# A recurrent attention with a max-out feed-forward on one core: the planner that orders the instructions gets other transfer rules and other due times

## The chip, the cores and the metric

One core of a Trainium2 chip. The metric is the device time of one launch in microseconds, median of several runs. Times that come from a view of the profile belong to one profiled execution.

## What is computed

The reference, cut to what matters. B, H, S, D are 4, 8, 768, 48:

```python
for t in range(S):
    cur = einsum('bhd,bhe->bhde', u * k[t], v[t])
    y[t] = einsum('bhd,bhde->bhe', r[t], state + cur)
    state = w * state + einsum('bhd,bhe->bhde', k[t], v[t])
x = y as (3072 tokens) x 384
h = max(x @ w1, x @ w2, x @ w3)          # 384 -> 768
out = h @ w_out                          # 768 -> 384
```

All inputs are float32. The kernel carries most products as pairs of 16-bit numbers, a high part and a low part.

## The kernel before

**Tiling.** The sequence is cut into 12 chunks of 64 positions. A chunk has two halves q of four heads each, so attention has 24 half-steps. A half-step loads `feat` (k and r, turned so that features lie on partitions; 512 KB) and `tok` (k, r and v by token; 576 KB), scales k and r by powers of the decay, and makes three groups of small matmuls on TensorE (line 438): *scores* (24 matmuls), *keys* (24, they update the state) and *values* (48, they give the chunk's x). The feed-forward (FFN) of a chunk follows: 162 matmuls *up* and 54 *down* (line 516), on 256 tokens, with ACT taking the first of three products, DVE the maximum with the other two (line 531), ACT the high part of h (line 534) and POOL or DVE its low part (line 540).

**Spread copies.** TensorE takes the 16-bit weights of attention as block-diagonal tiles. ACT writes the high part and DVE the low part into a dense tile (`kd`, `ktd`, `vd`, `sd`, lines 357, 362 and 364), and two DMAs on SP's queue (lines 344 and 345) copy its upper and lower partitions to the spread tile (`kb`, `ktb`, `vb`, `sb`). `kb` and `ktb`, and their dense tiles, exist once and serve both halves; `vb` and `sb` once for each half. `feat` has 2 buffers, `tok` 4. The scaled k lies in feat's own buffer, so `high` (line 357) and `low` (line 362) of k read that buffer.

**What sets the order.** Nothing is ordered by a scheduler at build time: every piece of work is given to `Plan.do` with an engine, a cost, what it reads and writes and a due time, and `Plan.order` runs a small model of the engines and of the DMA pipe. At each step it takes, of the pieces that could start soonest, the one with the least due time. The result is the order in which the instructions are issued, engine by engine; each engine works through its own list in that order, and SP through its DMAs. Two tables move due times: `SHIFT` by kind of work and by stage of the program (start, chunks up to 4, the rest), `ONCE` for single pieces. The model frees a buffer when the last piece that names it among what it reads, writes or takes is done.

In the model of before, a DMA of size bytes goes through one pipe of 275 GB/s, with 1.5 us before and 0.9 us behind; a pair of spread copies counts as one transfer. The pieces `kdh` and `kdl` (high and low of k) name the scaled k but not feat's buffer, so the model may free that buffer ahead of them. The program itself always waits for them: the next load into that buffer is held back until line 362 has read it.

**The rest.** At the start the eight weight tiles are loaded in sixteen halves and cut into high and low parts on ACT and DVE; near the end the sixteen halves are read again and vetted (lines 288 and 292), and all vets and sums of squares end in a flag that decides whether a slow general path runs.

Of the kernel before, what the change touches and what calls it, by code (L numbers as in the profile page):

```python
# [19 lines left out]
C = 64  # L20
# [5 lines left out]
U = 8  # L26
# [16 lines left out]
class Plan:  # L43
# [4 lines left out]
    ISSUE = {"sp": 0.45, "act": 0.45, "pool": 1.0}  # L48
    RATE, BEFORE, BEHIND = 275e3, 1.5, 0.9
    STAGES = (1.6, 4)  # L50
    SHIFT = {
        "act ah": (-52.95, 14.65, 8.9), "act am": (7.15, -25.65, 17.2), "act hh": (-9.55, -32.05, -3.85),
        "act his": (13, 6.75, -11.8), "act io": (-16.6, -18, 1.9), "act kb": (-22.35, -8.1, 1.25),
        "act kdh": (-90.3, 16.35, 22), "act ktb": (-2.95, -2, 18.3), "act ktdh": (17.9, 2.35, 12.8),
        "act m": (-43.35, -37.2, -5), "act odd": (-37.5, -41.9, 2.15), "act rh": (4.2, 20.15, -18.95),
        "act sdh": (-69.4, 17.1, -6.65), "act sq": (9.1, 22.1, -1.4), "act sqw": (52.2, 1.25, 16.95),
        "act sqx": (1.2, -35.65, -16.7), "act state": (-11.95, -53.65, -0.65), "act tkt": (-25.15, -0.3, 3.45),
        "act vb": (-38.6, 6.95, 36.75), "act vdh": (-6.55, 4.75, 38.8), "act xh": (-48.5, 27.05, 13.05),
        "act ztop": (-87.85, -53.05, -29.95), "dve a": (-2.75, 32.75, 52), "dve al": (25.3, -21.5, -38.65),
        "dve am": (-41.8, 17.75, -13.55), "dve ends": (5.75, 45, -4.95), "dve flag": (47.55, 0.5, -27.95),  # L60
        "dve good": (9.65, -41.8, 12.85), "dve hl": (13.7, -19.15, -51.75), "dve kT": (-41.9, 48, -0.3),
        "dve kdec": (17.3, 22.7, 20.85), "dve kdl": (-77.2, 31.3, -20.35), "dve ktdl": (-24.55, -30, -24.95),
        "dve lo": (-26.5, -32.1, 20.85), "dve m": (-48.25, -37.75, 4.15), "dve rT": (46.55, 22.2, 29.7),
        "dve rl": (-4.2, -8.6, 21.2), "dve sdl": (-11.9, 2.05, 25.1), "dve state": (-5.65, 12.5, 19.6),
        "dve vdl": (-13.05, 11.4, 22.45), "dve vet": (18.2, -10.95, 35.4), "dve word": (-32.05, 8.5, 49.3),
# [3 lines left out]
        "pool hl": (23.4, -2.9, -15.95), "pool kT": (6.85, -26.05, 38.8), "pool kdec": (2, -20.25, 12.7),  # L69
# [3 lines left out]
    }  # L73
    ONCE = {
        "act am": {3: -5.5}, "act his": {2: -61.15}, "act ktb": {1: -45.5}, "act ktdh": {3: -20.5},
        "act rh": {5: -30.5, 7: 29}, "act sdh": {3: 70}, "act sq": {3: -57, 5: -57, 6: -57.75, 39: -15}, "act xh": {0: 56.5},
        "act ztop": {3: 41.5}, "dve a": {2: -66.3}, "dve al": {4: -17}, "dve am": {5: -28.5, 6: -29.5, 8: -27.5},
        "dve hl": {2: -6}, "dve kT": {2: -29.5, 3: -27.5}, "dve kdec": {2: -86}, "dve ktdl": {8: 86.5},
        "dve lo": {3: -45, 4: -45, 5: -44.5, 6: 32.5}, "dve m": {13: 39.5}, "dve rT": {2: -117.5, 3: -116},
        "dve rl": {0: -65, 1: -63}, "dve sdl": {1: -57.5}, "dve state": {4: -25.5},  # L80
        "dve vdl": {0: -56, 2: 15, 5: -54.5, 6: -38.5}, "dve word": {4: -39.5, 5: -39.5, 6: -37}, "dve xl": {12: -39},
# [9 lines left out]
    def do(self, due, eng, cost, fn, reads=(), writes=(), takes=(), size=0, near=0):  # L91


        n = len(self.todo)
# [15 lines left out]
        self.todo.append(dict(n=n, due=due, eng=eng, cost=cost, fn=fn, need=need, takes=takes, size=size, near=near, kind=kind, touch={*reads, *writes, *new}))  # L110

    def order(self, free):

        free, pipe = dict(free), 0.0
# [14 lines left out]
        def earliest(p):  # L129
            t = free[p["eng"]]  # L130
            for m in p["need"]:
                q = self.todo[m]
                t = max(t, end[m] if q["eng"] != p["eng"] or q["size"] and not p["size"] else start[m] + busy[m] + (0 if p["size"] else 0.06))
            for pool, _ in p["takes"]:
                old = taken[pool]
                if len(old) >= self.bufs[pool]:
                    k = old[len(old) - self.bufs[pool]]
                    if left[k]:
                        return None
                    t = max(t, gone[k])  # L140
            return t

        while ready:
# [12 lines left out]
            start[n], free[e] = t, t + cost  # L156
            busy[n] = cost
            if p["size"]:
                pipe = max(pipe, t + p["cost"] + self.BEFORE) + p["size"] / self.RATE
                end[n] = pipe + self.BEHIND  # L160
            else:
                end[n] = t + cost + self.LAG[e]
# [16 lines left out]
def kernel(ctx, tc, feat, tok, wu, ut, ws, wo, cst, out):  # L179
# [514 lines left out]
    def dma(due, fn, size, reads=(), writes=(), takes=(), eng="sp", n=1):  # L694
        do(due, eng, n * Plan.ISSUE[eng], fn, reads, writes, takes, size)

# [40 lines left out]
    def before_scores(c, q, due):  # L737
# [5 lines left out]
        do(due - 0.26, "act", act(U * C), lambda: high(kd, u(raws[c, q]["kT"]), C), reads=[("kT", c, q)], writes=["kdh"])  # L743
        do(due - 0.24, "dve", dve(U * C), lambda: low(kd, u(raws[c, q]["kT"]), C), reads=[("kT", c, q), "kdh"], writes=["kdl"], near=1.2)
# [255 lines left out]
```

## Time and profile before

| what | value |
|---|---|
| median of 3 runs | 426.75 us (426.45 to 429.45) |
| the profiled execution | 427.69 us |
| its span, first to last instruction | 425.9 us |
| mean granted TensorE clock | 0.976 |
| instructions | 12008 |
| moved by DMA | 90.08 MB, mean 211 GB/s |

How to read the views: *idle* is the time of an engine ahead of an instruction, put down to what released it last. `PE` is matmul, `PEld` weight load, `SPq` the queue of DMAs that SP issues, `L438` a line of the kernel. `PE psa` is attention's work on TensorE, `PE psm` that of the FFN. In the groups of DMA issues the last number is the median time from the issue to the landing.

### The profile page before, as it was taken

The page shows a single profiled execution, that of the slowest core. Times are in us where ns is not written, and L with a number is a line of the kernel's source. Part 1 is how long each engine was busy: PE and PEld are TensorE (multiplying, and loading weights), DVE is VectorE, ACT ScalarE, POOL GpSimd, SP SyncE. Part 2 cuts the span into 40 slices and gives each one's busy share as a digit, 9 for nine tenths or more (in the row PEclk, how much of TensorE's full clock was granted, in tenths as well). Part 3 has the DMA queues.
Part 4 walks back from the last instruction along what each step waited for, and adds up shares of the span by engine and source line. Part 5 has one row for each costly group of instructions (what it writes and reads, how often), then busy time and mean ns, then how long its engine had stood idle before and what let it go on. Part 6 is the DMA issues. An engine that isn't in the chain of part 4 may idle for free.

```text
span 425.9 us, 12008 instructions
## 1 busy us (share of the span) xinstructions
PE 377.8 (89%) x4758; PEld 335.8 (79%) x4758; DVE 284.7 (67%) x550; ACT 274.9 (65%) x714; POOL 178.2 (42%) x180
## 2 busy tenths in 40 slices
PE   2969899989499999799898986986998999999995
PEld 2967679978389899788787875875887899888884
DVE  5889999896369678998683584574497643434340
ACT  5999988967266776685683574474476444689621
POOL 9000001495355288588467348526455501111020
PEclk9999999999979999999999898899999999999999
DMA  8956999976888996799879759649786793518101
GB/s 288 415 175 201 270 311 272 282 214 190 201 198 237 265 299 158 195 278 255 250 204 239 244 135 278 180 139 254 200 245 174 193 343 111 171 45 240 68 2 41
DMA packets 30954, 90.08 MB, mean 211 GB/s; under 512 B 4784, under 2 KB 9648, under 8 KB 30896
## 3 DMA queue, kind: packets, MB, share of 16 engines
q1 hardware_dynamic: 25568, 84.47, 68.9%
q10 hardware_dynamic: 5328, 4.82, 3.5%
q8 instruction: 38, 0.62, 0.6%
q14 instruction: 20, 0.16, 0.1%
HBM read 45.85 MB, written 4.72 MB: 119 GB/s over the span
## 4 chain that ended last, share of the span: by engine, by line
PE 35%; DMA 27%; DVE 16%; ACT 10%; issue 6%; POOL 2%; SPq 2%; ACTq 1%; DVEq 0%; POOLq 0%
PE psm L516 29%; DMA ktb<-ktd 10%; DMA kb<-kd 8%; PE psa L438 5%; DMA tok<-in_tok_dram 4%; ACT junk L378 3%; DVE m L531 2%; DMA out_dram<-io 2%; DVE w L276 2%; DMA feat<-in_feat_dram 2%; DVE raw L269 1%; DVE kd L362 1%; DVE al L458 1%; ACT ztop L265 1%; DVE feat L395 1%
## 5 line engine op out<-in xcount | busy, mean ns | idle before, releaser
L516 PEld LDWEIGHTS <-w 128*128 128x128 f16 x2592 | 253.7, 99 | 44.4 <-issue 10.0
L516 PE MATMUL psm<-xh,w 128*128 128x256 f16 x1296 | 228.6, 277 | 3.9 <-ACT xh L494 1.7
L516 PE MATMUL psm<-xl,w 128*128 128x256 f16 x648 | 157.6, 278 | 2.3 <-DVE xl L499 2.2
L540 POOL TENSOR_TENSOR hl<-m,hh 128x256 f16<-128x256 f32 x55 | 41.0, 748 | 164.0 <-ACT hh L534 162.7
L531 DVE SCALAR_TENSOR_TENSOR m<-psm,m 128x256 f32<-128x256 f32 x144 | 60.3, 420 | 52.2 <-PE psm L516 38.3
L395 POOL TENSOR_TENSOR feat<-feat,wrt 128x512 f32<-128x512 f32 x36 | 50.5, 1413 | 35.7 <-DMA feat<-in_feat_dram 35.7
L516 PE MATMUL psm<-hh,w 128*128 128x256 f16 x432 | 56.7, 275 | 2.3 <-ACT hh L534 2.3
L378 ACT ACTIVATE junk<-tok 128x384 bf16<-128x384 f32 x72 | 37.4, 520 | 26.4 <-DMA tok<-in_tok_dram 25.5
L534 ACT CAST hh<-m 128x256 f16<-128x256 f32 x72 | 28.5, 399 | 27.7 <-DVE m L531 27.0
L438 PE MATMUL psa<-al,vb 128*128 128x64 f16 x176 | 31.2, 193 | 3.8 <-DVE al L458 3.8
L516 PE MATMUL psm<-hl,w 128*128 128x256 f16 x216 | 34.0, 277 | 0.2
L438 PE MATMUL psa<-ah,vb 128*128 128x64 f16 x352 | 33.3, 193 | 0.3 <-ACT ah L453 0.3
L438 PEld LDWEIGHTS <-vb 128*128 128x128 f16 x528 | 29.2, 98 | 5.2 <-issue 4.7
L438 PE MATMUL psa<-rh,sb 128*128 128x64 f16 x352 | 32.5, 193 | 0.0
L438 PE MATMUL psa<-vd,ktb 128*128 128x48 f16 x480 | 16.2, 187 | 18.0 <-DMA ktb<-ktd 17.9
L527 ACT ACTIVATE m<-psm 128x256 f32<-128x256 f32 x72 | 26.9, 376 | 7.6 <-PE psm L516 7.3
L499 DVE SCALAR_TENSOR_TENSOR xl<-psa,xh 32x256 f16<-32x256 f32 (+2 forms) x60 | 28.3, 471 | 5.2 <-ACT xh L494 4.4
L494 ACT ACTIVATE xh<-psa 32x256 f16<-32x256 f32 (+2 forms) x60 | 24.9, 415 | 9.9 <-PE psa L438 4.4
L438 PE MATMUL psa<-rl,sb 128*128 128x64 f16 x176 | 31.2, 193 | 0.0
L405 DVE TENSOR_TENSOR rl<-feat,rh 128x512 f16<-128x512 f32 x22 | 21.8, 990 | 13.9 <-ACT rh L400 13.9
L438 PEld LDWEIGHTS <-ktb 128*128 128x128 f16 x480 | 15.0, 98 | 20.4 <-issue 12.0
L414 POOL TENSOR_TENSOR am<-tok,u_sb 128x384 f32<-128x384 f32 x18 | 20.0, 1109 | 24.0 <-DVE al L458 23.3
(93 smaller groups left out, 591.4 us busy)
## 6 DMA issues: line engine op xcount, KB each, us to landing
tok<-in_tok_dram SPq DMA_DIRECT2D x24, 576.0 KB, 7.2
raw<-in_ws_dram SPq DMA_DIRECT2D x24, 576.0 KB, 7.4
feat<-in_feat_dram SPq DMA_DIRECT2D x24, 512.0 KB, 4.5
kb<-kd SPq DMA_DIRECT2D x22, 256.0 KB, 6.9
kb<-kd SPq DMA_DIRECT2D x22, 248.0 KB, 6.8
ktb<-ktd SPq DMA_DIRECT2D x20, 256.0 KB, 6.7
ktb<-ktd SPq DMA_DIRECT2D x20, 248.0 KB, 7.1
raw<-in_wo_dram SPq DMA_DIRECT2D x8, 576.0 KB, 7.1
```

What stands on the lines that cost most here:

```text
L378: nc.scalar.activation(out=dst, in_=src, func=AF.Square, scale=scale, accum_out=stat[:, at:at + 1])
L395: helper(c).tensor_tensor(out=t[n], in0=t[n], in1=tb, op=ALU.mult)
L405: nc.vector.tensor_tensor(out=t["rl"], in0=units(t["rT"]), in1=t["rh"], op=ALU.subtract)
L414: helper(c).tensor_tensor(out=w.rearrange("p (g b) d -> p g b d", g=2), in0=t["r"], in1=by_token(u_sb, q), op=ALU.mult)
L438: nc.tensor.matmul(out=ps, lhsT=l[i], rhs=rr[j], start=first and n == 0, stop=last and n == 2)
L494: nc.scalar.mul(out=hi, in_=src, mul=SC_X)
L499: nc.vector.scalar_tensor_tensor(out=lo, in0=src, scalar=SC_X, in1=hi, op0=ALU.mult, op1=ALU.subtract)
L516: nc.tensor.matmul(out=ps, lhsT=a, rhs=b, start=first and n == 0, stop=last and n == len(prods) - 1)
L527: nc.scalar.mul(out=m, in_=ps, mul=SC_M)
L531: nc.vector.scalar_tensor_tensor(out=m, in0=ps, scalar=SC_M, in1=m, op0=ALU.mult, op1=ALU.max)
L534: nc.scalar.copy(out=h[0][:, f, :], in_=m)
L540: lows_by(c, f).tensor_tensor(out=h[1][:, f, :], in0=m, in1=h[0][:, f, :], op=ALU.subtract)
```

## The change

The change is in the planner and in what three pieces declare; no instruction is added or taken away. (1) `high` and `low` of k now name feat's buffer among what they read. (2) At most eight transfers are under way in the model: a DMA starts no sooner than the eighth before it has ended, and the two copies of a spread are modelled one by one. (3) The rates differ by kind: 300 GB/s for loads, 220 for spreads, 500 for stores; issue costs and the times before and behind are a little smaller. (4) Both tables of due times are new, and due times are rounded to whole steps of 0.0001 before they are compared. The diff, with one row of each table:

```diff
-    ISSUE = {"sp": 0.45, "act": 0.45, "pool": 1.0}
-    RATE, BEFORE, BEHIND = 275e3, 1.5, 0.9
+    ISSUE = {1: 0.4, 2: 1.1}
+    LOAD, SPREAD, STORE = 300e3, 220e3, 500e3
+    BEFORE, BEHIND, LANES = 1.3, 0.8, 8
...
-        "act ah": (-52.95, 14.65, 8.9), "act am": (7.15, -25.65, 17.2), "act hh": (-9.55, -32.05, -3.85),
+        "act ah": (-9.7, -6.55, -15.55), "act am": (-7.65, -25.3, 6.4), "act hh": (-8.7, -29.65, -23.6),
...
-        "sp word": {1: 0.05, 8: -0.1},
+        "pe va": {4: -10, 10: -1.5, 16: -0.3}, "sp word": {9: -0.2, 10: 0.1, 14: -0.12},
...
-    def do(self, due, eng, cost, fn, reads=(), writes=(), takes=(), size=0, near=0):
+    def do(self, due, eng, cost, fn, reads=(), writes=(), takes=(), size=0, near=0, parts=1):
...
-        self.todo.append(dict(n=n, due=due, eng=eng, ...
+        self.todo.append(dict(n=n, due=math.floor(due * 1e4 + 0.5), eng=eng, ...
...
-        free, pipe = dict(free), 0.0
+        free, pipe, lanes = dict(free), 0.0, [0.0] * self.LANES
...
+            if p["size"]:
+                t = max(t, lanes[-self.LANES])
...
-            start[n], free[e] = t, t + cost
-            busy[n] = cost
-            if p["size"]:
-                pipe = max(pipe, t + p["cost"] + self.BEFORE) + p["size"] / self.RATE
-                end[n] = pipe + self.BEHIND
-            else:
-                end[n] = t + cost + self.LAG[e]
+            start[n], now = t, t
+            for _ in range(p["parts"] if p["size"] else 0):
+                now = max(now, lanes[-self.LANES]) + cost / p["parts"]
+                pipe = max(pipe, now + self.BEFORE) + p["size"] / p["parts"]
+                lanes.append(pipe + self.BEHIND)
+            free[e] = now if p["size"] else t + cost
+            end[n] = lanes[-1] if p["size"] else t + cost + self.LAG[e]
+            busy[n] = free[e] - t
...
-        do(due, eng, n * Plan.ISSUE[eng], fn, reads, writes, takes, size)
+        do(due, eng, Plan.ISSUE[n], fn, reads, writes, takes, size / (Plan.STORE if eng == "act" else Plan.SPREAD if n > 1 else Plan.LOAD), parts=n)
...
-        do(due - 0.26, "act", ..., reads=[("kT", c, q)], writes=["kdh"])
-        do(due - 0.24, "dve", ..., reads=[("kT", c, q), "kdh"], writes=["kdl"], near=1.2)
+        do(due - 0.26, "act", ..., reads=[f, ("kT", c, q)], writes=["kdh"])
+        do(due - 0.24, "dve", ..., reads=[f, ("kT", c, q), "kdh"], writes=["kdl"], near=1.2)
...
-        do(due - 0.29, "act", 1.25, ..., reads=[("kT", c, q)], writes=["kb"])
+        do(due - 0.29, "act", 1.25, ..., reads=[f, ("kT", c, q)], writes=["kb"])
```

**What moves.** Every engine's order changes from its first rows on; lines of the changed kernel are numbered 5 higher. The prediction rests on three places.

First, SP's queue from the load of feat of the tenth half-step on, whose slot is that of the eighth. Before:

```order
L204 DMA feat<-in_feat_dram 128x1024
L344 DMA sb_153<-sd 64x1536
L345 DMA sb_153<-sd 64x1488
L344 DMA ktb<-ktd 64x2048
L345 DMA ktb<-ktd 64x1984
L209 DMA tok<-in_tok_dram 128x1152
L344 DMA vb_139<-vd_147 64x1536
L345 DMA vb_139<-vd_147 64x1488
L344 DMA kb<-kd 64x2048
L345 DMA kb<-kd 64x1984
```

The same pieces in the change:

```order
L349 DMA ktb<-ktd 64x2048
L350 DMA ktb<-ktd 64x1984
L349 DMA vb_139<-vd_147 64x1536
L350 DMA vb_139<-vd_147 64x1488
L349 DMA sb_153<-sd 64x1536
L350 DMA sb_153<-sd 64x1488
L209 DMA feat<-in_feat_dram 128x1024
L349 DMA kb<-kd 64x2048
L350 DMA kb<-kd 64x1984
L214 DMA tok<-in_tok_dram 128x1152
```

The load of feat moved from ahead of the copies of sb, ktb and vb to behind them; it still stands just ahead of kb.

Second, SP's queue around the load of feat of the 22nd half-step, whose slot is that of the 20th. Before:

```order
L344 DMA sb_155<-sd 64x1536
L345 DMA sb_155<-sd 64x1488
L204 DMA feat<-in_feat_dram 128x1024
L209 DMA tok<-in_tok_dram 128x1152
L344 DMA ktb<-ktd 64x2048
L345 DMA ktb<-ktd 64x1984
L344 DMA sb_153<-sd 64x1536
L345 DMA sb_153<-sd 64x1488
L344 DMA kb<-kd 64x2048
L345 DMA kb<-kd 64x1984
```

In the change:

```order
L349 DMA kb<-kd 64x2048
L350 DMA kb<-kd 64x1984
L349 DMA vb_141<-vd_149 64x1536
L350 DMA vb_141<-vd_149 64x1488
L349 DMA sb_155<-sd 64x1536
L350 DMA sb_155<-sd 64x1488
L209 DMA feat<-in_feat_dram 128x1024
L214 DMA tok<-in_tok_dram 128x1152
L349 DMA ktb<-ktd 64x2048
L350 DMA ktb<-ktd 64x1984
```

The kb in both lists is that of the 20th half-step, ktb too; kb moved from behind the load of feat to ahead of it.

Third, TensorE where attention ends, at the last values matmuls (`sb_155`). Before, the next work is FFN up:

```order
L438 MATMUL psa<-rl,sb_155 128x64
L438 LDWEIGHTS sb_155
L438 MATMUL psa<-rh,sb_155 128x64
L516 LDWEIGHTS w_105
L516 MATMUL psm<-xh,w_105 128x256
```

In the change it is the down part of the chunk before the last:

```order
L443 MATMUL psa<-rl,sb_155 128x64
L443 LDWEIGHTS sb_155
L443 MATMUL psa<-rh,sb_155 128x64
L521 LDWEIGHTS w_110
L521 MATMUL psm<-hh,w_110 128x256
```

Behind this point stand 621 FFN matmuls in the order of before (135 up, 54 down, 171 up, 54 down, 153 up, 54 down) and 270 in the change (54 down, 162 up, 54 down). Behind the last scores stand 648 and 450.

More of the change, by code (lines that the diff above doesn't have):

```diff
@@ L1 @@
+import math
 from contextlib import ExitStack
@@ L47 @@
     LAG = {"pe": 0.25, "dve": 0.1, "act": 0.2, "pool": 0.15}
-    ISSUE = {"sp": 0.45, "act": 0.45, "pool": 1.0}
-    RATE, BEFORE, BEHIND = 275e3, 1.5, 0.9
+    ISSUE = {1: 0.4, 2: 1.1}
+    LOAD, SPREAD, STORE = 300e3, 220e3, 500e3
+    BEFORE, BEHIND, LANES = 1.3, 0.8, 8
     STAGES = (1.6, 4)
     SHIFT = {
-        "act ah": (-52.95, 14.65, 8.9), "act am": (7.15, -25.65, 17.2), "act hh": (-9.55, -32.05, -3.85),
[L53 to L65, printed above, removed]
[3 rows of a table removed]
-        "pool hl": (23.4, -2.9, -15.95), "pool kT": (6.85, -26.05, 38.8), "pool kdec": (2, -20.25, 12.7),
[3 rows of a table removed]
@@ new lines @@
+        "act ah": (-9.7, -6.55, -15.55), "act am": (-7.65, -25.3, 6.4), "act hh": (-8.7, -29.65, -23.6),
+        "act his": (-2.45, -21.15, -5.8), "act io": (-5.95, -0.45, -1.35), "act kb": (-2.25, -0.45, 2.8),
+        "act kdh": (-86.7, 14.7, 4.25), "act ktb": (-52.35, -7.15, 1.35), "act ktdh": (-3.95, 3.15, -16.65),
+        "act m": (-40.8, -10.6, 2.3), "act odd": (-7.1, -20.9, 11.4), "act rh": (-9.45, 10.75, 2.8),
+        "act sdh": (-26.9, 10.05, -4.75), "act sq": (-13.5, 11.4, 2.25), "act sqw": (3.8, 23, 5.6),
@@ new lines @@
+        "act sqx": (2.6, -1.8, -12.15), "act state": (-26.85, -4.5, 4.35), "act tkt": (-7.4, -7.95, 23.65),
+        "act vb": (-7.4, 9.35, 19.65), "act vdh": (-15.6, -0.35, -3.6), "act xh": (-8.9, -12.75, 5),
+        "act ztop": (-25.95, -22.7, -2.15), "dve a": (-8.35, -2.8, 21.5), "dve al": (-5.85, -35.85, -10.35),
+        "dve am": (-21.65, -2.25, 41.55), "dve ends": (16.5, 18.05, -15.05), "dve flag": (9.85, -15.45, 14.05),
+        "dve good": (-4.75, -1.25, 2.85), "dve hl": (3.3, 5.85, 12.85), "dve kT": (-35.75, -25.2, 4.25),
@@ new lines @@
+        "dve kdec": (-3.8, -14.4, 17.25), "dve kdl": (-84.1, -12.1, 1.2), "dve ktdl": (-6.85, 7.35, -5.9),
+        "dve lo": (8.4, 1.65, 13.2), "dve m": (-21.1, -35.4, -12.75), "dve rT": (4.7, -2.4, 6.9),
+        "dve rl": (-1.65, -14.9, -9.85), "dve sdl": (24.2, -11.4, 29.1), "dve state": (11.2, 14.15, 9.9),
+        "dve vdl": (-8.3, -13.55, 3.35), "dve vet": (-29.9, -9, -18.1), "dve word": (-11.05, -17.7, 22.4),
[3 rows of a table added]
+        "pool hl": (-18.95, -42.75, 12.05), "pool kT": (0.45, -20.75, 7.85), "pool kdec": (8.9, 0.2, 13.55),
[3 rows of a table added]
@@ L73 @@
     }
     ONCE = {
[L75 to L79, printed above, removed]
@@ L80 @@
-        "dve rl": {0: -65, 1: -63}, "dve sdl": {1: -57.5}, "dve state": {4: -25.5},
-        "dve vdl": {0: -56, 2: 15, 5: -54.5, 6: -38.5}, "dve word": {4: -39.5, 5: -39.5, 6: -37}, "dve xl": {12: -39},
[4 rows of a table removed]
+        "act ah": {0: -5.5, 2: 7.5}, "act am": {0: -23, 1: -8.5}, "act hh": {2: 7.5, 8: -6},
+        "act his": {0: -25.5, 3: -25, 4: -28, 6: -16, 7: -7.5}, "act ktdh": {0: -25}, "act rh": {0: -21.5, 1: -20},
+        "act sq": {8: -17.5, 9: -17.5, 10: -18, 14: -16.5}, "act sqx": {0: -20.5}, "act vdh": {0: -15.5},
@@ new lines @@
+        "act xh": {0: -16, 1: -21.5}, "act ztop": {2: -2.5, 4: 26, 9: 17}, "dve a": {2: -56.5, 3: -57},
+        "dve am": {2: 26.5, 3: 27, 6: -43, 8: -44}, "dve hl": {1: -63}, "dve kT": {2: -29}, "dve ktdl": {1: -47},
+        "dve lo": {4: -73.5, 9: -68, 10: -62.5, 11: -62.5}, "dve m": {6: -32.7, 7: -33}, "dve rT": {2: -69.5},
+        "dve state": {0: -70.5}, "dve word": {6: -54, 11: -48.5}, "dve xl": {14: -10},
+        "pe dn": {0: 65.5, 8: -4, 9: -4, 10: -3, 16: 0.5, 17: -3, 22: 13.5, 45: 13.5}, "pe ke": {5: -6, 10: 3.7, 12: 2},
@@ L109, in do @@
         need.discard(n)
-        self.todo.append(dict(n=n, due=due, eng=eng, cost=cost, fn=fn, need=need, takes=takes, size=size, near=near, kind=kind, touch={*reads, *writes, *new}))
+        self.todo.append(dict(n=n, due=math.floor(due * 1e4 + 0.5), eng=eng, cost=cost, fn=fn, need=need, takes=takes, size=size, near=near, parts=parts, kind=kind, touch={*reads, *writes, *new}))
     def order(self, free):
-        free, pipe = dict(free), 0.0
+        free, pipe, lanes = dict(free), 0.0, [0.0] * self.LANES
         left = {}
@@ L742, in before_scores @@
         do(due - 0.30, h, cost, lambda: scale(c, q, "rT"), reads=[f], writes=[("rT", c, q)], near=0.55)
-        do(due - 0.26, "act", act(U * C), lambda: high(kd, u(raws[c, q]["kT"]), C), reads=[("kT", c, q)], writes=["kdh"])
-        do(due - 0.24, "dve", dve(U * C), lambda: low(kd, u(raws[c, q]["kT"]), C), reads=[("kT", c, q), "kdh"], writes=["kdl"], near=1.2)
+        do(due - 0.26, "act", act(U * C), lambda: high(kd, u(raws[c, q]["kT"]), C), reads=[f, ("kT", c, q)], writes=["kdh"])
+        do(due - 0.24, "dve", dve(U * C), lambda: low(kd, u(raws[c, q]["kT"]), C), reads=[f, ("kT", c, q), "kdh"], writes=["kdl"], near=1.2)
         dma(due - 0.22, lambda: spread(nc.sync, kb, kd, C), 524288, reads=["kdh", "kdl"], writes=["kb"], n=2)
@@ L775, in first_scores @@
         do(due - 0.30, "dve", dve(U * C), lambda: scale(c, q, "kT"), reads=[f], writes=[("kT", c, q)], near=0.55)
-        do(due - 0.29, "act", 1.25, lambda: apart(kb, units(raws[c, q]["kT"]), C), reads=[("kT", c, q)], writes=["kb"])
+        do(due - 0.29, "act", 1.25, lambda: apart(kb, units(raws[c, q]["kT"]), C), reads=[f, ("kT", c, q)], writes=["kb"])
         do(due - 0.28, "dve", dve(U * C), lambda: scale(c, q, "rT"), reads=[f], writes=[("rT", c, q)], near=0.55)
```

2 lines of the change are left out of this document (added), and 15 rows, old and new, of tables (ONCE, SHIFT).

## The prediction

> **What bounds the kernel now.** I read the page's first line, then the windows, then who waited for whom on TensorE and on the SP queue, then the chain that ended last. The span and the busy times by stage come first; the columns of the second fence are the stretch, its length, the busy time of PE, PEld, DVE, ACT and POOL, the granted clock, the DMA share and GB/s.
>
> ```profile
> span 425.9 us, 12008 instructions
> ```
>
> ```profile
> 0.00:40.00 40.00, 27.30 (x149) 24.50 (x150) 31.96 (x63) 33.78 (x80) 10.41 (x19) 1.00 0.76 265
> 40.00:100.00 60.00, 55.98 (x763) 49.29 (x761) 56.18 (x105) 49.64 (x131) 18.38 (x16) 1.00 0.93 269
> 100.00:125.00 25.00, 18.50 (x184) 15.70 (x183) 11.34 (x22) 13.02 (x39) 11.31 (x13) 0.86 0.82 205
> 125.00:225.00 100.00, 94.13 (x1445) 84.96 (x1443) 82.05 (x150) 68.61 (x183) 63.77 (x60) 1.00 0.84 235
> 225.00:300.00 75.00, 63.24 (x851) 54.73 (x848) 42.38 (x81) 41.02 (x112) 41.85 (x39) 0.91 0.76 206
> 300.00:353.00 53.00, 50.54 (x760) 45.89 (x758) 34.23 (x60) 28.22 (x73) 22.62 (x22) 1.00 0.76 228
> 353.00:421.00 68.00, 68.00 (x629) 60.76 (x625) 26.44 (x70) 40.27 (x98) 9.84 (x15) 1.00 0.33 103
> ```
>
> TensorE is the bound, and it is unevenly fed. From 353 to 421 us it never stops. Before that it is idle for 12.7 us up to 40 us, where ACT is busy 33.8 of 40 us, and for 4.02 + 6.50 + 5.87 + 11.76 + 2.46 = 30.6 us from 40 to 353 us. The second sum is the one the change can reach. Its causes, and the SP queue's own longest wait:
>
> ```profile
> PE psa L438 <- DMA ktb<-ktd: 17.9, 8, 6.0
> PE psa L438 <- DVE al L458: 3.8, 5, 1.6
> PE psa L438 <- DMA kb<-kd: 2.0, 4, 1.1
> ```
>
> ```profile
> SPq L204 <- DVE kd L362: 62.3, 13, 9.6
> ```
>
> Of 30.6 us, 17.9 + 2.0 = 19.9 us are waits for the spread copies ktb and kb; 10.7 us are small waits on other engines. SP stood 62.3 us, 13 times, at a load of feat whose slot was still read by the subtraction that makes the low part of k (line 362). SP issues in order, so every copy behind such a load stood too. The two dearest places:
>
> ```profile
> 97.47 0.59 SPq L345 DMA_DIRECT2D kb<-kd  x1
> 107.74 0.33 SPq L204 DMA_DIRECT2D feat<-in_feat_dram  x1
> 109.32 0.99 SPq L344 DMA_DIRECT2D ktb<-ktd  x1
> ...
> 276.59 0.59 SPq L345 DMA_DIRECT2D sb<-sd  x1
> 286.83 0.33 SPq L204 DMA_DIRECT2D feat<-in_feat_dram  x1
> 287.85 0.47 SPq L344 DMA_DIRECT2D ktb<-ktd  x1
> 291.94 0.59 SPq L344 DMA_DIRECT2D kb<-kd  x1
> ```
>
> ```profile
> 117.54 1.12 PE L438 MATMUL psa<-vd,ktb 128*128 128x48 f16 x24 [6.01 <-DMA ktb<-ktd]
> 295.65 0.81 PE L438 MATMUL psa<-vd,ktb 128*128 128x48 f16 x24 [3.89 <-DMA ktb<-ktd]
> ```
>
> SP is silent from 98.1 to 107.7 and from 277.2 to 286.8 us; ktb leaves at 109.3 and 287.9, and TensorE idles 6.01 and 3.89 us for it. Each long idle is also followed by a stretch at half clock:
>
> ```profile
> 115.31:122.14 6.83, 4.60 (x42) 3.58 (x43) 3.77 (x7) 2.76 (x7) 3.72 (x5) 0.50 1.02 241
> 234.78:238.19 3.41, 3.41 (x24) 2.49 (x23) 1.46 (x3) 1.78 (x5) 0.00 (x0) 0.50 0.44 120
> 262.08:268.91 6.83, 5.81 (x65) 4.79 (x66) 5.99 (x10) 4.57 (x13) 4.27 (x4) 0.50 0.60 159
> 296.22:299.63 3.41, 3.41 (x24) 2.47 (x21) 3.04 (x6) 2.27 (x7) 2.67 (x3) 0.50 0.82 193
> ```
>
> In these, TensorE worked 4.60 + 3.41 + 5.81 + 3.41 = 17.2 us at half speed, so half of it, 8.6 us, was lost. The reach of the change from 40 to 353 us is 30.6 + 8.6 = 39.2 us.
>
> **The change part by part.** No arithmetic, no buffer and no byte changes: the list of instructions is the same, in another order. So the sum has only waits, and where TensorE's work stands.
>
> *FFN work moved forward.* The end of the chain of waits gives the prices of a block (start, duration, how many):
>
> ```profile
> 334.23 0.70 PE psa L438 x24
> ...
> 351.77 1.40 PE psa L438 x48
> 353.17 67.81 PE psm L516 x621
> ...
> 421.00 0.38 ACT io L553
> ```
>
> A matmul of the FFN costs 67.81 / 621 = 0.1092 us, scores or keys 0.70, values 1.40. In the order of before, 621 FFN matmuls stand behind the last values; in the change, 270. So 351 of them, 38.3 us, are moved from the full stretch at the end to places between attention blocks. That is nearly the reach of 39.2 us, so the move gains what the earlier idle can take in, and nothing of itself. Counting by these prices, consecutive scores blocks from the fifth to the last stood 229.1 / 19 = 12.1 us of TensorE work apart, and stand 251.2 / 19 = 13.2 apart now.
>
> *Waits for kb and ktb, 19.9 us.* One buffer holds each, so a refill can't start before the matmuls that read it: 0.70 us for the block, 0.5 for the issue, and then the landing:
>
> ```profile
> kb<-kd SPq DMA_DIRECT2D x22, 256.0 KB, 6.9
> ktb<-ktd SPq DMA_DIRECT2D x20, 256.0 KB, 6.7
> ```
>
> That makes 8.1 us at least. Where two such blocks stand nearer than that in TensorE work, TensorE must wait. By the order, in before the shortfalls are 2.1 us (scores) and 4.0 us (keys), in the change 2.7 (7.5 and 6.0 us apart) and 2.3 (7.9 and 6.0): 6.1 us then, 5.0 now. So 19.9 - 6.1 = 13.8 us of the waits came from elsewhere, and the places above say from where: the queue behind feat. In the change the loads of feat stand behind sb and ktb at the first place and behind kb at the second, but in most rounds one still stands just ahead of the kb that waits for the same subtraction. I keep a third, 4.6 us (bounds: all 13.8 or nothing). Left are 5.0 + 4.6 = 9.6, gained 10.3 us (bounds 1.1 to 14.9).
>
> *Half clock, 8.6 us.* Three of the four stretches follow a ktb wait, the one at 234.8 a wait of TensorE for other work. I scale with the kb and ktb waits: 8.6 x 9.6 / 19.9 = 4.1 left, 4.5 gained (bounds 0 to 7). The Trainium skill, "TensorE: Matmul & The Clock Gate", Part 1, says that the clock falls to half after an idle window of about 3.4 us and comes back after as much work. The trace agrees on 6.01 and 3.89 us; the stretch at 234.8 follows a shorter idle, and the page says that the window runs free. By the page, a change that leaves no idle over 3.4 us would give back the whole 8.6 instead of 4.5, and the sum would be some 4 us lower.
>
> *Other waits, 10.7 us.* The row for al and the smaller ones belong to single meetings of two engines in the old order. The new order has meetings of its own, which no row shows. Bounds: all gone, or as many more (21.4). As more TensorE work now stands between attention blocks, I take half gone: 5.4 gained.
>
> *Start, 12.7 us.* The first weight now comes behind both first pairs of feat and tok, and ACT does two more pieces ahead of the second half of the first xh. ACT is nearly full there, so this is hidden by nothing; a square sum costs 0.7 us with its read-out (row below). I take 0, bounds -2 to +3.
>
> ```profile
> 160.83 0.63 ACT junk L378 x2
> ```
>
> *End.* The last values are now followed by 54 matmuls of the FFN of the step before, 5.9 us, which covers ACT's and DVE's leaving of x; five of the sixteen weight re-reads stand on SP ahead of the last kb, vb and sb, but 20 us of TensorE work lie between the scores that let the kb copy ahead of them go and those after which the last kb may go. Cost 0; without this cover, the landing of one copy, 6.9 us.
>
> Sum: 10.3 + 4.5 + 5.4 = 20.2 us. The profiled execution took 427.69 us (span 425.9 and 1.8 around it): 427.7 - 20.2 = 407.5. Its time is 0.9 above the median of the runs, 426.75, so I forecast a median of **406.5 us**.
>
> A second way round: the last scores began at 347.96 us, and 648 FFN matmuls stood behind them; 450 do now.
>
> ```profile
> 347.96 0.19 PE L438 MATMUL psa<-rh,kb 128*128 128x64 f16 x1
> ```
>
> If attention merely arrives when it did, the end comes 198 x 0.1092 = 21.6 us sooner, less one values block of 1.4 that is now behind: 20.2 us. Both ways meet.
>
> **Rivals.**
> - *TensorE becomes the only bound.* All of 14.9 + 7 + 10.7 = 32.6 us comes back: 394. For it: DMA share falls to 0.76 in the poorest stretches. Against: 5 us of shortfalls, and a feat load still at the head of most rounds.
> - *The idle travels along.* The moved FFN work pushes the attention blocks back by its own length, as the loop of one kb copy to the next runs through SP, ACT and DVE whatever TensorE does: the end stays, 426 (423 to 430). For it: 13 waits at feat remain possible. Against: the two places above.
> - *The loop is the bound, and gets longer (slower).* Copies of kb, the fourth and the twentieth of 22, left at
>
> ```profile
> 81.02 0.46 SPq L344 DMA_DIRECT2D kb<-kd  x1
> ...
> 317.18 2.03 SPq L344 DMA_DIRECT2D kb<-kd  x1
> ```
>
>  which is 236.2 / 16 = 14.8 us a step, over the 13.2 that TensorE now has. At this pace the last kb leaves at 81.0 + 18 x 14.8 = 347.4, lands 6.9 later, and 450 x 0.1092 + 0.7 + 2.8 = 52.6 us of work, 4.9 us of closing and 1.8 around follow: 413.6. The decision lies at 15.6 us a step, where this gives 428. One microsecond more, 16.6, gives 446. For it: kb now often stands behind a fresh feat of 512 KB, and sometimes tok. The Trainium skill, "DMA: Bandwidth & Descriptors", Queues, rings and completion order, says that each DMA engine takes the descriptors of a ring in order, so those bytes come first; no row here separates that. Against: in before kb had feat, tok, sb and ktb ahead of it in the same burst, as at 286.8 to 291.9.
> - *Nothing of what it says.* The added reads don't matter if kd was never late in the new due times; then only the due times act, which is the second rival's time.
>
> **How the numbers follow.** Forecast with partial return, 398 to 418: 0.62. TensorE alone the bound: 0.08. Loop at its old pace, 413.6, inside the first range: 0.07. Idle travels: 0.11. Longer loop: 0.12. A difference under 1%, 4.3 us, can't be told from none here. Faster by over 1%: 0.77; within 1%: 0.11; slower: 0.12. The range takes in the other cases down to 394 and up to 426: about 0.17 is left out, most of it above.
>
> **What would show it.** Right: SP's wait at line 204 (209 there) for the subtraction under 30 us; TensorE's wait for ktb under 8 us; idle from 40 us to the last values under 22 us; granted clock over 0.98; last values at about 370 to 375 us, with 29.5 us of FFN behind. Wrong: the last values after 390 us, or TensorE waiting for kb or ktb in nearly every round.

## The result, and the profile after

The changed kernel takes **400.55 us** (median of 4 runs, 395.96 to 404.61). Beside it the kernel before took 428.1 us (4 runs, 426.45 to 430.89). The ratio is 0.9315, with a 95% interval of 0.921 to 0.9419. The forecast was 406.5 us, with a range of 394 to 426. The profiled execution of the changed kernel took 400.71 us. Runs that lay more than 1.5% above the fastest of their kernel are left out of every ratio in this text, but not out of the medians.

First come the page's span and its busy times. In the kernel before, PE was busy 377.8 us of a span of 425.9.

```profile
span 398.9 us, 12009 instructions
...
PE 369.8 (93%) x4758; PEld 332.6 (83%) x4758; DVE 280.4 (70%) x550; ACT 275.2 (69%) x714; POOL 179.6 (45%) x180
```

The span is 27.0 us shorter. (The page of before counts 12008 instructions; the two traces differ in semaphore instructions alone, which follow from the order.) With the same 4758 matmuls PE is busy 8.0 us less, mostly by its clock, and idle 398.9 - 369.8 = 29.1 us instead of 48.1, which is 19.0 less. The windows show in which stages. The columns are those of the prediction; the first, the last and the sum of the middle rows matter.

```profile
0.00:40.00 40.00, 26.83 (x139) 23.88 (x140) 31.91 (x64) 33.09 (x79) 10.41 (x19) 1.00 0.89 312
40.00:100.00 60.00, 54.49 (x728) 47.48 (x726) 53.74 (x101) 49.90 (x131) 14.24 (x13) 1.00 0.81 232
100.00:125.00 25.00, 24.75 (x351) 22.30 (x349) 17.83 (x32) 16.91 (x48) 20.45 (x19) 1.00 0.91 261
125.00:225.00 100.00, 95.54 (x1332) 86.33 (x1333) 72.67 (x139) 64.41 (x174) 60.77 (x59) 0.98 0.84 223
225.00:300.00 75.00, 74.88 (x1080) 68.33 (x1079) 56.75 (x105) 50.78 (x140) 51.88 (x47) 1.00 0.93 242
300.00:366.00 66.00, 65.37 (x883) 59.50 (x881) 37.41 (x79) 48.30 (x118) 18.41 (x20) 1.00 0.73 226
```

From 40 us to the last values TensorE is idle for 5.51 + 0.25 + 4.46 + 0.12 + 0.63 = 11.0 us, where it was 30.6. The stage from 225 to 300 us, which had lost 11.76, loses 0.12. The first 40 us lose 13.2 (12.7 before). The waits of TensorE from 40 to 365 us, all that concern attention:

```profile
PE psa L443 <- DMA vb<-vd: 2.3, 2, 1.8
...
PE psa L443 <- DMA sb<-sd: 1.7, 2, 1.2
...
PE psa L443 <- DVE al L463: 1.5, 2, 1.1
PE psa L443 <- DMA kb<-kd: 0.6, 1, 0.6
```

ktb, which had 17.9 us, has no row any more, and kb has 0.6. The SP queue, from 60 to 366 us:

```profile
SPq L349 <- PE psa L443: 41.1, 19, 10.0
SPq L349 <- DVE kd L367: 30.5, 6, 12.2
...
SPq L209 <- DVE kd L367: 6.7, 5, 3.1
```

SP still waits a lot, but at another instruction. It stood 62.3 us at loads of feat (line 204 then, 209 now) for the subtraction, and stands 6.7. It now stands at the spread copies (line 349) for what they need themselves: the end of the matmuls that read the old tile, and the dense tile. What stands behind such a copy waits too, but by the rows above little of it reaches TensorE. The end of the chain that ended last:

```profile
335.60 5.29 DMA kb<-kd
...
341.02 0.86 PE psa L443 x24
341.88 14.74 PE psm L521 x135
...
364.33 29.49 PE psm L521 x270
```

The last scores begin at 341.02 us, 6.9 us sooner than before (347.96), and 450 FFN matmuls stand behind them.

### The profile page after: what moved, and what is told of

The parts are those of the page before. It is cut to its first block, busy times and chain, and to the rows that moved or that the text cites. A ratio compares the mean times of both kernels' runs of the same rounds, so it can differ in the third digit from the quotient of the medians.

```text
span 398.9 us, 12009 instructions
## 1 busy us (share of the span) xinstructions
PE 369.8 (93%) x4758; PEld 332.6 (83%) x4758; DVE 280.4 (70%) x550; ACT 275.2 (69%) x714; POOL 179.6 (45%) x180
## 4 chain that ended last, share of the span: by engine, by line
PE 58%; DMA 13%; ACT 11%; DVE 10%; issue 4%; SPq 1%; POOL 1%; ACTq 0%; DVEq 0%; POOLq 0%
PE psm L521 48%; PE psa L443 9%; DMA sb<-sd 4%; DMA kb<-kd 3%; ACT junk L383 3%; DMA tok<-in_tok_dram 2%; DMA raw<-in_wo_dram 2%; DVE m L536 2%; ACT ztop L270 1%; DVE w L281 1%; ACT am L431 1%; DVE feat L400 1%; DMA ktb<-ktd 1%; ACT w L277 1%; ACT xh L499 1%
## 5 line engine op out<-in xcount | busy, mean ns | idle before, releaser
L521 PE MATMUL psm<-xh,w 128*128 128x256 f16 x1296 | 225.2, 275 | 5.6 <-ACT xh L499 2.9
L521 PE MATMUL psm<-xl,w 128*128 128x256 f16 x648 | 155.0, 274 | 3.4 <-DVE xl L504 3.2
L545 POOL TENSOR_TENSOR hl<-m,hh 128x256 f16<-128x256 f32 x55 | 43.4, 790 | 148.1 <-ACT hh L539 146.9
L539 ACT CAST hh<-m 128x256 f16<-128x256 f32 x72 | 28.7, 399 | 33.5 <-DVE m L536 30.6
L400 POOL TENSOR_TENSOR feat<-feat,wrt 128x512 f32<-128x512 f32 x36 | 47.8, 1344 | 6.3 <-DMA feat<-in_feat_dram 3.5
L383 ACT ACTIVATE junk<-tok 128x384 bf16<-128x384 f32 x72 | 37.3, 518 | 10.5 <-DMA tok<-in_tok_dram 8.0
L443 PEld LDWEIGHTS <-sb 128*128 128x128 f16 x528 | 27.7, 98 | 1.9 <-DMA sb<-sd 1.3
L367 DVE TENSOR_TENSOR kd<-feat,kd 128x512 f16<-128x512 f32 x22 | 19.9, 905 | 8.7 <-ACT kd L362 7.6
L433 POOL TENSOR_TENSOR am<-cs,a 128x512 f32<-128x512 f32 x18 | 22.4, 1242 | 6.8 <-DVE a L424 6.8
```

What stands on the lines that cost most here:

```text
L383: nc.scalar.activation(out=dst, in_=src, func=AF.Square, scale=scale, accum_out=stat[:, at:at + 1])
L400: helper(c).tensor_tensor(out=t[n], in0=t[n], in1=tb, op=ALU.mult)
L433: helper(c).tensor_tensor(out=t["a"], in0=eye.unsqueeze(1).broadcast_to([P, U, C]), in1=t.pop("sum").unsqueeze(2).broadcast_to([P, U, C]), ...
L443: nc.tensor.matmul(out=ps, lhsT=l[i], rhs=rr[j], start=first and n == 0, stop=last and n == 2)
L521: nc.tensor.matmul(out=ps, lhsT=a, rhs=b, start=first and n == 0, stop=last and n == len(prods) - 1)
L539: nc.scalar.copy(out=h[0][:, f, :], in_=m)
```

## The experiments

After the two traces had been read there were two theories. The **slot theory**: the old model believed feat's buffer free before the subtraction had read it, so it ordered everything for a feat that could not come yet; the gain is the end of that. The **placement theory**, its rival: the new due times put FFN work between attention blocks, and this by itself pulls the end in. The expectations below call them queue theory and place theory; the first was then held more narrowly, with SP's standing at loads of feat as the loss itself. Times below are medians; each ratio is to the kernel before on the same chip, whose median is given for each group.

### First group: the parts alone (before: 429.32 us)

**b_feat3**: the kernel before with a third buffer for feat. The order is the same, the slot is just never late.

```diff
-        f = raw.tile([P, 2, 2, B, C], F32, name="feat", bufs=2)
+        f = raw.tile([P, 2, 2, B, C], F32, name="feat", bufs=3)
```

> The kernel before with a third buffer for feat and the same order of every engine. A load of feat then waits for the low part of k of three half-steps ago, which is long done. Queue theory (the loss before came from SP standing at feat loads, 62.3 us in 13 waits): SP's wait at line 204 for line 362 falls below 5 us, TensorE's wait for ktb from 17.9 to below 8, and the time by about 13 us or more with the half clock, to 408 to 416 us. Place theory (the gain comes from where the FFN matmuls stand between attention blocks, 351 of them moved from the end): the waits move to other places and the time stays above 421 us.

Measured: **402.62 us**, ratio 0.9362 (0.9277 to 0.9447), below the 408 to 416 us that the slot theory had given. The views are of an execution of 406.3 us, the longest of four. Its SP queue has no wait at feat for the subtraction; the longest row of line 204 is the first below. Then its window up to the last values, and the end of its chain:

```profile
SPq L204 <- DMA kb<-kd: 1.7, 1, 1.7
```

```profile
40.00:331.97 291.97, 275.84 (x3993) 249.07 (x3991) 227.53 (x417) 201.11 (x537) 159.21 (x147) 0.99 0.90 248
```

```profile
330.57 1.40 PE psa L438 x48
331.97 67.81 PE psm L516 x621
```

All 621 FFN matmuls still stand behind the last values, in the same 67.81 us. But the last values end at 331.97 instead of 353.17, and TensorE's idle time up to there is 291.97 - 275.84 = 16.1 us instead of 30.6. One more buffer, without any of the change, gives a time that the interval does not tell from that of the change. So the late slot was what the kernel before lost by; moved FFN work is not needed for the gain.

**b_newtables**: the kernel before with the new tables of due times, and nothing else of the change. One row of the table for all:

```diff
-        "act ah": (-52.95, 14.65, 8.9), "act am": (7.15, -25.65, 17.2), "act hh": (-9.55, -32.05, -3.85),
+        "act ah": (-9.7, -6.55, -15.55), "act am": (-7.65, -25.3, 6.4), "act hh": (-8.7, -29.65, -23.6),
```

> The kernel before with only the two tables of due times of the change; model, rates and declared reads as before. In its order 216 FFN matmuls stand behind the last values (621 before, 270 in the change), and feat loads still stand ahead of the low part of k that they wait for. Place theory: most of the gain is there, 400 to 410 us. Queue theory: SP still stands at feat loads for more than 30 us, TensorE waits for ktb or kb more than 10 us, and the time is 412 to 425 us.

Measured: **435.5 us**, ratio 1.0142 (1.0078 to 1.0206). Both theories had given a gain, and the kernel is slower by 1.4%. Only 216 FFN matmuls stand behind the last values, fewer than in the change (the chain's last FFN row, first below, has all but one of them). The placement theory falls here: the positions alone bring no gain. The slot is still late, and TensorE still waits for ktb:

```profile
404.03 25.28 PE psm L516 x215
```

```profile
SPq L204 <- DVE kd L362: 23.6, 7, 8.7
```

```profile
PE psa L438 <- DMA ktb<-ktd: 9.5, 5, 3.9
PE psa L438 <- DMA kb<-kd: 5.0, 5, 2.0
```

**b_read**: the kernel before with the three declared reads only.

```diff
-        do(due - 0.26, "act", ..., reads=[("kT", c, q)], writes=["kdh"])
-        do(due - 0.24, "dve", ..., reads=[("kT", c, q), "kdh"], writes=["kdl"], near=1.2)
+        do(due - 0.26, "act", ..., reads=[f, ("kT", c, q)], writes=["kdh"])
+        do(due - 0.24, "dve", ..., reads=[f, ("kT", c, q), "kdh"], writes=["kdl"], near=1.2)
...
-        do(due - 0.29, "act", 1.25, ..., reads=[("kT", c, q)], writes=["kb"])
+        do(due - 0.29, "act", 1.25, ..., reads=[f, ("kT", c, q)], writes=["kb"])
```

> The kernel before with only the three declared reads of feat's buffer added; its model and its old due times stay. The FFN behind the last values is 621 matmuls as before. Queue theory: SP's wait at feat loads for the low part of k falls to under a third of 62.3 us, and the time to 408 to 420 us. Place theory: no more than 1% faster, 423 us or above, since the tables were made for another order.

Measured: **413.53 us**, ratio 0.9663 (0.9566 to 0.976). Three words in the old model, with the old rates and tables, give about 15 us.

```profile
SPq L204 <- DVE kd L362: 14.8, 7, 5.4
```

SP's wait at feat is down from 62.3 to 14.8 us, and the gain is a little over half of that of the third buffer.

**a_noread**: the change without these three reads.

```diff
-        do(due - 0.26, "act", ..., reads=[f, ("kT", c, q)], writes=["kdh"])
+        do(due - 0.26, "act", ..., reads=[("kT", c, q)], writes=["kdh"])
...
```

> The changed kernel without the three declared reads; its rates, eight lanes and due times stay, and 270 FFN matmuls stand behind the last values as in the change. Queue theory: SP again stands at feat loads (over 25 us at line 209 for line 367, against 6.7 in the change), TensorE's waits for kb and ktb return to over 6 us from 0.6, and the time rises to 406 to 418 us. Place theory: 398 to 405 us, no more than the spread of the change's own runs.

Measured: **432.26 us** (10 runs), ratio 1.0059 (1.0011 to 1.0107), far above the 406 to 418 us that the slot theory had given. Without the reads the change gains nothing, though its 270 FFN matmuls behind the last values are the same:

```profile
SPq L209 <- DVE kd L367: 42.3, 6, 12.2
```

```profile
399.21 29.49 PE psm L521 x270
```

The last values end at 399.21 us instead of 364.33 (in an execution of 434.99 us). This is the rival "the idle travels along" of the prediction, seen pure: 351 matmuls, 38.3 us, moved forward, and the end of attention pushed back by that and 7.7 us more, against 353.17 before.

### Second group: how a late slot costs (before: 431.45 us)

The prediction had said how: SP issues in order, so the copies behind a waiting feat stand too. **b_feat_later** takes that away. The order is that of before, but each load of feat from the ninth on is moved directly ahead of the kb copy that waits for the same subtraction, or ahead of the first work on that feat if this stands sooner.

```diff
...
+    for step in range(8, len(loads)):
+        load = loads[step]
+        spot = min(order.index(copies[step - 4]), order.index(scales[(step // 2, step % 2)]))
+        if order.index(load) < spot:
+            order.remove(load)
+            order.insert(spot - 1, load)
```

> The kernel before, two feat buffers, every engine's own order as before, except that on SP each load of feat from the ninth half-step on stands directly ahead of the kb copy that waits for the same subtraction (line 362). Theory of the held copies (ktb, sb and vb that were ready stood behind a waiting feat load): TensorE's wait for ktb falls from 17.9 below 8 us, and the time comes near that of the third buffer, 402 to 412 us. Theory of the late feat (the load itself came too late for POOL and for the next k): POOL still waits for feat more than 25 us, and the time stays at 418 us or above.

Measured: **434.25 us** (10 runs), ratio 1.0054 (1.0008 to 1.01). My theory of the held copies falls as the whole cause. Its first step came true: TensorE's wait for ktb is gone, 17.9 to 2.2 us. Yet others came in its place. The first row below is of the kernel before, the others of b_feat_later.

```profile
POOL feat L395 <- DMA feat<-in_feat_dram: 35.7, 10, 8.9
...
POOL feat L395 <- DMA feat<-in_feat_dram: 55.8, 12, 12.1
PE psa L438 <- DMA kb<-kd: 7.6, 4, 2.9
PE psm L516 <- DVE m L531: 6.8, 5, 2.9
PE psm L516 <- ACT m L527: 6.8, 2, 6.2
PE psa L438 <- DVE al L458: 4.3, 6, 1.7
PE psa L438 <- DMA ktb<-ktd: 2.2, 2, 1.4
```

TensorE no longer waits for ktb, but feat still comes when its slot is free, which is after the time that the order was made for. POOL, whose list has the scaling of feat at a fixed place, stands there, and DVE's and ACT's pieces come late to TensorE's FFN. So I read these rows: in one order SP met the late slot first, in the other POOL did, and the time is the same within 1%. SP does not run free either. It stands at the copies for their own dense tiles instead: for that of ktb 35.8 us, where it was 15.8.

```profile
SPq L344 <- DVE ktd L362: 35.8, 13, 7.4
```

The move also costs feat something. The median from issue to landing, of the kernel before and of b_feat_later:

```profile
feat<-in_feat_dram SPq DMA_DIRECT2D x24, 512.0 KB, 4.5
...
feat<-in_feat_dram SPq DMA_DIRECT2D x24, 512.0 KB, 6.3
```

So the run shows that taking the copies out from behind feat gains nothing in all. What held copies cost with a feat in time, it does not show.

**a_feat3**: the change with a third buffer for feat (the edit of b_feat3, at line 208).

> The changed kernel with a third buffer for feat, order as in the change. Queue theory: the change has already taken the waits out (6.7 us at feat loads, 0.6 us of TensorE waiting for kb, none for ktb), so the time stays within 1% of the change, 397 to 404 us. If its remaining 3 waits for loads in front of kb still cost, it falls below 396 us.

Measured: **400.13 us**, ratio 0.9264 (0.9184 to 0.9344): the same as the change. What the buffer gave to the old order (26 to 27 us) it does not give to the new one, since the new one hardly meets a late slot (6.7 us in 5 waits).

**a_nolanes**: the change with the limit on transfers under way lifted out of reach.

```diff
-    BEFORE, BEHIND, LANES = 1.3, 0.8, 8
+    BEFORE, BEHIND, LANES = 1.3, 0.8, 64
```

> The changed kernel whose model allows 64 transfers under way in place of 8; reads, rates and due times as in the change. If the lane rule carries a part of the gain, more copies are issued ahead of their time, TensorE waits for kb and ktb over 5 us again and the time is above 406 us. If the reads alone carry it, 398 to 405 us.

Measured: **414.76 us**, ratio 0.9607 (0.9533 to 0.968), 14 us over the change.

```profile
SPq L209 <- DVE kd L367: 28.0, 6, 10.9
```

```profile
PE psa L443 <- DMA kb<-kd: 5.4, 5, 2.9
```

With another limit the same tables make another order, and that order meets the slot again. So this does not say that eight is a property of the chip. It says that the tables and the model belong together.

**b_newtables_read**: the kernel before with the new tables and the three reads, but its old rates and no limit.

> The kernel before with the new tables and the three declared reads, but the old rates and no lanes. Queue theory with reads as the whole cause: SP's wait at feat loads under 20 us and 405 to 415 us, near the 413.5 us of old tables with the reads. If the tables fit only the new rates and lanes, as the 435.5 us of the new tables alone suggest, it stays above 418 us.

Measured: **432.63 us** (10 runs), ratio 1.0002 (0.9954 to 1.0049). The reads gave 15 us with the old tables, and with the new ones under old rates about 3 (435.5 to 432.6). The change has the same tables and the same reads and takes 400.55 us. So with these tables its transfer rules (rates, issue costs, the limit, the two copies modelled one by one), with the rounding of due times, are worth about 32 us, as much as the reads. Of the issue costs, that of a single DMA is smaller in the new rules (0.4 instead of 0.45 us), that of a pair larger (1.1 instead of 0.9).

```profile
SPq L204 <- DVE kd L362: 16.2, 5, 8.2
```

```profile
PE psa L438 <- DMA ktb<-ktd: 9.8, 7, 3.8
PE psa L438 <- DMA kb<-kd: 9.6, 6, 3.7
```

### Third group: what a wrong order costs beyond the slot (before: 427.93 us)

**a_noread_feat3**: a_noread with a third buffer (both edits are shown above).

> The changed kernel without the three reads, 432.3 us with two feat buffers, now with three and in the same order. Late feat theory: the model's belief that the slot is free ahead of the low part of k becomes true, and the 32 us come back: 398 to 408 us. If the order without the reads is worse for another reason, it stays above 418 us.

Measured: **411.47 us**, ratio 0.9597 (0.9512 to 0.9682). That lies between the two expected ranges. Of the 31.7 us that the reads are worth in the change (432.26 - 400.55), the buffer gives back about 20; the times come from three sets of runs, whose kernels before differ by up to 1.4 us. The other 11 or so I put down to the order itself, which was made by a model that was wrong on the slot; no row shows it.

**b_newtables_feat3**: b_newtables with a third buffer.

> The kernel before with the new tables, old rates, no lanes and no reads, 435.5 us with two feat buffers, now with three in the same order. If the slot of feat is the whole of what the old model had wrong, 400 to 410 us. If the old rates and the missing lanes cost too, as the 414.8 us of the change without lanes say, 412 to 425 us.

Measured: **430.58 us**, ratio 1.0104 (1.0003 to 1.0206), above both expected ranges. Little comes back, although no load of feat waits for the subtraction. POOL still waits for feat:

```profile
POOL feat L395 <- DMA feat<-in_feat_dram: 22.9, 5, 15.8
```

Here the slot is not the cause; which rate or which due time is, stays open.

**a_notables**: the change with both tables empty.

```diff
...
+    SHIFT = {}
+    ONCE = {}
```

> The changed kernel, new model and reads, with both tables of due times empty, so the due times written in the program alone order it. If the right model alone makes the gain, 400 to 412 us. If the tables carry a part that was fitted to this model, more than 415 us, and more idle time of TensorE spread over many small waits.

Measured: **407.4 us**, ratio 0.9499 (0.9403 to 0.9595). The new model with no fitted due time at all gives some 21 of the 27 us; the tables add about 7 (407.4 to 400.55, from two sets of runs; the two intervals of the ratio just overlap). POOL waits longest for feat here of all kernels,

```profile
POOL feat L366 <- DMA feat<-in_feat_dram: 75.3, 6, 66.3
```

of which 66.3 us are one wait, up to 77.3 us, for POOL's first scaling of feat. The row says when POOL began, not what that cost: no wait of TensorE up to there names POOL. So a wait of POOL for feat is no price by itself, and in b_feat_later the price is read from TensorE's rows, not from POOL's. The views are of the longest of four executions, 413.45 us; from 40 to 82 us TensorE is idle for 12.1 us of it, behind kb, weights and x.

**b_feat3_held**: meant to give the old order an early feat and held copies together, by a third buffer with the copies of ktb, sb and vb moved from behind feat to behind the next kb.

```diff
...
+        for p in [p for p in order[here:there] if p["kind"] in ("sp ktb", "sp sb", "sp vb")][::-1]:
+            order.remove(p)
+            order.insert(order.index(spread_k) + 1, p)
```

> The kernel before with a third feat buffer, so that feat arrives early, but with the copies of ktb, sb and vb that stood behind a load of feat now standing behind the kb copy that follows it, which waits for the same subtraction (line 362) as the load did. So the copies are held about as long as before, and only feat is early. Held copies theory: TensorE waits for ktb over 10 us and the time is above 418 us. Late feat theory (the order was made for a feat that comes when the model says): POOL's wait for feat below 20 us and the time at 400 to 412 us.

Measured: 6168.05 us, which says nothing on either theory. The launch went down the slow general path, whose 3072 matmuls of line 650 are on its page. The likely reason is that the edit put copies behind pieces that read their tiles; no view shows that. What held copies cost with an early feat is left open.

### The kernels in one table

PE busy and idle are from the first row of each page: idle is span less busy. They and SP's wait belong to the profiled execution, whose time is given; the median is of all runs. In a_notables SP stands 13.1 us at loads of feat for another reader of the slot, the low part of r.

| kernel | PE busy | PE idle | SP at feat for the subtraction | profiled execution | median |
|---|---|---|---|---|---|
| before | 377.8 | 48.1 | 62.3 | 427.69 | 428.1 |
| b_feat_later | 379.5 | 51.0 | 20.9 | 432.32 | 434.25 |
| b_newtables | 379.9 | 54.4 | 23.6 | 436.09 | 435.5 |
| b_newtables_read | 381.5 | 51.5 | 16.2 | 434.8 | 432.63 |
| b_newtables_feat3 | 376.5 | 47.7 | none | 425.94 | 430.58 |
| a_noread | 381.9 | 51.3 | 42.3 | 434.99 | 432.26 |
| a_nolanes | 376.3 | 37.3 | 28.0 | 415.37 | 414.76 |
| b_read | 373.0 | 39.3 | 14.8 | 414.11 | 413.53 |
| a_noread_feat3 | 375.3 | 34.8 | none | 411.88 | 411.47 |
| a_notables | 375.6 | 36.1 | none | 413.45 | 407.4 |
| b_feat3 | 371.2 | 33.2 | none | 406.3 | 402.62 |
| after | 369.8 | 29.1 | 6.7 | 400.71 | 400.55 |
| a_feat3 | 368.8 | 28.6 | none | 399.23 | 400.13 |

The work is the same in all of them, and so the time is TensorE's idle time and, behind it, its clock. SP's wait at feat does not order the kernels: b_feat_later has a third of it, b_newtables_feat3 none, and neither is faster than before. It was the sign of the cause in the kernel before, not the price.

## Why the prediction was right, point by point

- **What bounds the kernel**: right. TensorE's idle and half clock between 40 us and the last values were the reach (39.2 us), and the gain came out of them: idle 30.6 to 11.0, and half clock 8.6 to 1.7. The start lost 0.5 us more (0 was said, bounds -2 to +3), the end cost nothing.
- **FFN work moved forward gains nothing of itself**: right. b_newtables and a_noread move it and gain nothing; b_feat3 does not and gains all. The second way of the prediction (what stands behind the last scores) is a balance of positions: 20.2 us for the moved work, and 347.96 - 341.02 = 6.9 for attention that came sooner, together 27.1. Such a balance always closes. What the prediction put into it, that attention arrives when it did, was 6.9 us off, and so it was chance that both ways met at 20.2.
- **Waits for kb and ktb**: sign right, size off. 9.6 us were to be left, and 0.6 are. The part that failed is the 5.0 us of shortfalls. I took 8.1 us as the least distance of two blocks that share a tile, with the median landing of before, 6.9 us. The page of the change has

```profile
kb<-kd SPq DMA_DIRECT2D x22, 256.0 KB, 5.7
...
ktb<-ktd SPq DMA_DIRECT2D x20, 256.0 KB, 6.4
```

 and the last kb landed in 5.29 us (chain above). A median of the old order was no floor for another order. I read it as having the queueing of its own order in it.
- **"The queue behind feat", 13.8 us, of which a third was to stay**: this step failed as a mechanism. b_feat_later took the copies out from behind feat, TensorE's wait for ktb went, and the time did not. The 13.8 us were one face of a late slot: with the copies ahead, other waits took their place (of FFN for DVE and for ACT, 6.8 us each). What held copies cost by themselves stays open. The prediction gave the added reads no term of the sum; a_noread says that 31.7 us hang on them.
- **Other waits**: half gone, 5.3 left, was said; 11.0 - 0.6 = 10.4 us are left, nearly all before 100 us (5.51) and between 125 and 225 us (4.46). Of these, 4.0 us are waits for the copies of vb and sb, for which TensorE had no row in the kernel before: meetings of the new order, which the term had named and not sized. So it promised 5.1 us too much, and that for kb and ktb 9.0 too little.
- **Half clock**: 4.1 us were to be left, 1.7 are: one stretch of 3.41 us.

```profile
124.33:127.74 3.41, 1.63 (x54) 1.43 (x50) 3.23 (x7) 1.70 (x6) 2.38 (x3) 1.00 1.04 248
127.74:131.15 3.41, 3.41 (x34) 2.67 (x31) 3.40 (x5) 2.80 (x8) 2.83 (x3) 0.50 0.98 236
```

 The variant that the prediction drew from the Trainium skill, "TensorE: Matmul & The Clock Gate", Part 1 (no idle over 3.4 us, no half clock, the whole 8.6 us back), came nearer in its number, but the stretch here speaks against its rule: the idles ahead of it were of 0.57 and 1.21 us. More on this below.
- **Sum**: 20.2 us was said and 27.0 came, from 427.69 to 400.71 in the profiled executions. By terms, kb and ktb gave 9.0 more, the clock 2.4 more, other waits 5.1 less, the start 0.5 less: 5.8 of the 6.8. For the rest, PE's busy time fell by 8.0 us where the half-clock stretches account for 6.9. So the forecast was helped by luck: misses of both signs came together, and its range, 394 to 426, took in most of its rivals.
- **Rivals.** TensorE as the only bound, 394, lies nearly as near to the result (6.6 us) as the forecast does (6.0): what is left of the reach is 11.0 idle and 1.7 of clock. The loop of kb copies at its old pace, and the longer loop, fell. In the change the fourth and the twentieth kb copy left at

```profile
83.61 0.47 SPq L349 DMA_DIRECT2D kb<-kd  x1
...
301.20 0.46 SPq L349 DMA_DIRECT2D kb<-kd  x1
```

 which is 217.6 / 16 = 13.6 us a step, not 14.8, and close to the 13.2 us of TensorE's work. In b_feat3, which has the order of before, the same copies left at 81.91 and 294.83 us, 13.3 us a step. So the loop had been slow because of the slot, and 14.8 was no bound. "The idle travels along" is what happens without the reads (a_noread). "Nothing of what it says" fell with it: the added reads matter as much as any part, though the transfer rules matter as much (b_newtables_read).
- **The signs named**: SP at feat for the subtraction under 30 us (6.7), ktb under 8 us (none), idle under 22 us (11.0), clock over 0.98 (0.994), 29.5 us of FFN behind the last values (29.49) all came. Last values at 370 to 375 us did not: they end at 364.33, sooner by about what the sum fell short.

What the change did, then: it told the model the truth about one slot, and the order made from it hardly runs into that slot. Shown by b_read (15 us from the reads alone), a_noread (nothing without them) and b_feat3 (the same gain with a slot that is never late). The reads are not the whole of it: with the new tables they need the new transfer rules too (b_newtables_read gains nothing, a_nolanes about half). Open: why the new tables under old rates lose even with a third buffer. Not tried: the old model without any tables, which would say what the old tables were worth, and the new rules with the old tables.

## What to carry to other kernels

When a queue stands at a load whose buffer is still being read, give that tile one more buffer first, without touching the order: it takes one number (and here 512 KB), and says what the wait costs. It gave 27 us with the order of before (b_feat3) and hardly anything where the order had other faults (b_newtables_feat3). Where a planner makes the order, each piece must name every buffer that it reads, or the order is made for an arrival that cannot happen. Due times that go with one model need not suit another: those of the change, in the old model, cost some 6 us (b_newtables). A wait that disappears is no gain until the end of the chain has moved: b_feat_later lost 15.7 us of TensorE's longest wait and not a microsecond of time.

## What the runs showed of the hardware

The half clock came after less idle than I had expected, and by a rule that the traces show well. In each trace the half-clock stretches of the loop are 3.41 us long or a multiple of it, and they lie on one grid of that step. I counted, for 13 profiled executions from 40 us to the end, how long TensorE was busy in each cell of the grid at full clock. Of the cells with at most 1.50 us of 3.41 busy, 34 of 34 were followed by half clock. Between 1.51 and 1.67 us it was 11 of 19. Above that, none of more than 1260 was. Three cells of the kernel before that led to half clock, and one that did not:

```profile
231.36:234.77 3.41, 1.36 (x12) 0.91 (x10) 1.22 (x3) 2.43 (x7) 0.83 (x1) 1.00 0.96 225
258.67:262.08 3.41, 1.13 (x11) 0.77 (x8) 0.55 (x1) 2.00 (x7) 3.16 (x5) 1.00 1.04 269
292.80:296.21 3.41, 0.56 (x23) 0.59 (x24) 0.88 (x3) 2.28 (x8) 1.47 (x2) 1.00 1.03 236
91.42:94.83 3.41, 1.80 (x52) 1.69 (x50) 3.41 (x3) 0.00 (x0) 3.41 (x3) 1.00 0.49 113
```

So it is not one idle of 3.4 us that costs the clock here, but a cell of the grid in which TensorE is idle for a little more than half, in one piece or in several. A cell so lost costs up to 1.7 us, half of the 3.41 behind it where TensorE has work all through, and two short waits in one cell can cost it, as the 0.57 and 1.21 us in the changed kernel did. Busy times are modelled at the ends of matmuls, so the limit is known to some 0.1 us only.
